# Cluster-masked attention and a maxout FFN: pairs of heads on two halves of the partitions, FFN blocks of 256 tokens

## The chip, the core and the metric

The kernel runs on one core of one Trainium2 chip. The core has five engines that run side by side, each through its own list of instructions in order: TensorE (PE) multiplies matrices, VectorE (DVE), ScalarE (ACT) and GpSimd (POOL) work element by element, and SyncE (SP) issues transfers to 16 DMA engines. PE writes to PSUM, in banks of 512 float32 columns; DVE and ACT read it. The metric is the time of one execution on the device in microseconds, lower is better.

## The reference, cut to what matters

```
B, H, S, D = 4, 8, 768, 64;  16 clusters;  FFN 512 -> 768 -> 512, three-way maxout
q_assign = argmax(q_n . c_n);  k_assign = argmax(k_n . c_n)        # per row and head
scores   = q k^T / sqrt(D), and -1e9 where q_assign != k_assign
attn     = exp(scores - max);  attn = attn / (sum + 1e-9)
x        = attn v, heads side by side                              # 3072 x 512
out      = max(x w1, x w2, x w3) w_out                             # weights are float64
```

## The kernel before, in words

Float32 products are split into parts so that PE's faster formats give nearly the whole precision: q and k into two float32r parts (`hi` and `lo`), probabilities, values, x and the hidden values into two float16 parts.

A pair of heads is prepared by `qk_prep`: both heads' q over k are loaded (q on the lower 64 partitions, k on the upper), ACT makes `hi` (L362), POOL or DVE makes `lo` (L365), and `qk_moves` shifts k's parts to the lower and q's to the upper half by DMA within SBUF (L370 to L372), so that one matmul over 128 partitions adds two products of parts. `cluster_scores` and `cluster_rows` find the cluster of each row and put one-hot rows below `q hi` and `k hi`, by DMA (L448).

The step of the attention is `scores`: one head, one tile of 128 queries. Two matmuls of 512 and 256 columns (L475), two more (L477), then a chain over engines: the row maximum on DVE (L480, written back scaled), the exponential with its row sum on ACT (L483), the factor 1/sum on DVE (L484, L485), the high part on ACT (L493) and the low part on DVE (L494). For some heads POOL splits instead (L489 to L491, chosen by `by_pool`). A DMA transpose turns both parts into `pt` (L495). There are 192 steps. `av` multiplies three tiles of `pt` with v (L505, L508), `x_split` makes two parts of x on POOL.

The FFN goes by blocks of 384 tokens (`ffn_units`): 18 groups of 12 matmuls (L546), whose results ACT and DVE fold into a maximum (L556, L558), POOL splits it (L564, L565), and three output tiles of 18 matmuls each (L580, L589, L591).

`spread` and `at_prio` give each piece a priority by the step it belongs to; a list scheduler puts the instructions of each engine into a fixed order by these. The first batch goes through its heads twice, half of the queries at a time, so that the FFN starts early; the FFN of a batch runs beside the attention of the next, the last one alone. The weights are converted from float64 on the chip (`convert`) during the first quarter of the program. PSUM holds three `big` tiles of two banks for scores and two `one` tiles of one bank for all else.

Of the kernel before, what the change touches and what calls it, by code (L numbers as in the profile page):

```python
# [8 lines left out]
F32 = mybir.dt.float32  # L9
# [7 lines left out]
AX = mybir.AxisListType  # L17
PSUM = bass.MemoryType.PSUM
# [5 lines left out]
def kernel(  # L24
# [23 lines left out]
    nc = tc.nc  # L48
    B, H, D, S = qk.shape
    D = D // 2  # L50
    C = cent.shape[0] // H
    P = 128
    QT = S // P
    NPAIR = H // 2
# [4 lines left out]
    G = 3  # L59
    AGAIN = {(0, 0), (1, 0)}  # L60
    NB = G * P
    NG = QT // G

# [4 lines left out]

    dpool = ctx.enter_context(tc.tile_pool(name="dr", bufs=2, space=bass.MemoryType.DRAM))
# [7 lines left out]
    def stage():  # L77
        return sb.tile([P, S], F32, tag="stage", name="stage", bufs=3)

# [1 line left out]
    fp = [ctx.enter_context(tc.tile_pool(name="ffn", bufs=2))]  # L81
    tctx = ExitStack()
    tp = tctx.enter_context(tc.tile_pool(name="first", bufs=1))
    ident = tp.tile([P, P], F32, name="ident")
# [6 lines left out]
    onehot = cpool.tile([P, S // 32, 32], F32, name="onehot")  # L91
    nc.gpsimd.memset(onehot, 0.0)
    cw = cpool.tile([P, H, P], F32R, name="cw")
    nc.gpsimd.memset(cw.bitcast(F32), 0.0)

    def pow2_scale(cols, name):
        """p: the power of two at or below the largest magnitude; s = 2^14 / p; on all partitions."""
# [13 lines left out]
    # A load that would run too far ahead is held back to the last step of the attention that  # L111
    # has been issued: one element of its tile is first written from the sums of that step.
    pace = []

    def hold(x):
        if pace:
            nc.gpsimd.tensor_copy(x, pace[-1])

    last = {}

    def behind(what, f, *args):
        with tc.issue_after(last[what].ins):
            f(*args)

# [6 lines left out]
    def centroids(c_sb):  # L131
# [3 lines left out]
        sq = tp.tile([P, D], F32, name="sq")  # L135
# [13 lines left out]
        c2 = tp.tile([P, 2, D], F32, name="c2")  # L149
# [4 lines left out]
        tv = t[:, 0:P].rearrange("p (h c) -> p h c", c=C)  # L154
        cv = cw.rearrange("p (r i) x -> p r i x", i=2)
        tv = tv.rearrange("p (r i) c -> p r i c", i=2)
        parts = []
        for a in range(2):
            rows = slice(D * a, D * a + D)
            for i in range(2):  # L160
                at = D * a + 32 * i
                parts.append((tv[rows, :, i, :], cv[rows, :, i, at : at + C], cv[rows, :, i, at + C : at + 2 * C]))
        for x, hi, lo in parts:
            last["cw_hi"] = nc.scalar.copy(hi, x)
        for x, hi, lo in parts:
            last["cw_lo"] = nc.vector.tensor_tensor(lo, x, hi.bitcast(F32), op=ALU.subtract)

# [8 lines left out]
    JA = 4  # L176
    w16 = [cpool.tile([P, JA, 2, 3, CT, P], F16, name="w16a")]
    wo16 = []
# [4 lines left out]
    top = [cpool.tile([P, DM], I32, name="top")]  # L183
    nc.gpsimd.memset(top[0], 0)

    def convert(wp, src, a, d):
        """src: int16 quarters of float64 in DRAM [P, a, 4m]; d: float32 [P, a * m] on chip."""
        n = d.shape[-1]
        x = wp.tile([P, n + 1, 4], I16, tag="wd", name="wd", bufs=2)
        hold(x[0:1, 0, 0:2].bitcast(F32))  # L190
        xf = x.rearrange("p n w -> p (n w)")
        nc.sync.dma_start(out=xf[:, 1 : 1 + 4 * n].rearrange("p (a m) -> p a m", a=a), in_=src)
        up = top[0]
        nc.scalar.copy(up.bitcast(F16).rearrange("p (n w) -> p n w", w=2)[:, 0:n, 1], x[:, 1:, 0].bitcast(BF16))
        low = x[:, 0:n, 2:4].bitcast(I32).rearrange("p n w -> p (n w)")
        nc.vector.scalar_tensor_tensor(
            d.bitcast(I32), low, 13, up[:, 0:n], op0=ALU.logical_shift_right, op1=ALU.bitwise_or
        )
# [10 lines left out]
    def w_units(wp, jt):  # L209
# [4 lines left out]
        def load(i):  # L214
            def f():
                if not i:
                    got["x"] = wp.tile([P, 3 * n], F32, tag="wf", name="wf", bufs=2)
                w = (w1, w2, w3)[i].bitcast(I16).rearrange("(c p) n -> p c n", p=P)
                src = w[:, :, 4 * jt * P : 4 * (jt + 1) * P]
                convert(wp, src, CT, got["x"][:, i * n : (i + 1) * n])  # L220
# [9 lines left out]
        def split(i):  # L230
            def f():
# [3 lines left out]
                    w16[jt // JA][:, jt % JA, 0, i].rearrange("p c n -> p (c n)"),  # L235
                    w16[jt // JA][:, jt % JA, 1, i].rearrange("p c n -> p (c n)"),
# [7 lines left out]
    def wo_units(fp):  # L244
        got = []

        def part(jt):
            def f():
                wp = fp[0]
                w = w_out.bitcast(I16)[jt * P : (jt + 1) * P, :]  # L250
                if jt % 3 == 0:
                    got[:] = [wp.tile([P, 3 * DM], F32, tag="wf", name="wf", bufs=2)]
                x = got[0][:, jt % 3 * DM : (jt % 3 + 1) * DM]
                convert(wp, w.rearrange("p (a n) -> p a n", a=1), 1, x)
# [8 lines left out]
                split16(x, s, wo16[0][:, jt, 0], wo16[0][:, jt, 1], WO_SPLIT[jt])  # L263
# [3 lines left out]
        def common():  # L267
# [9 lines left out]
            for jt in range(JT):  # L277
                t = wo16[0][:, jt].rearrange("p a n -> p (a n)")
# [6 lines left out]
    vmax = cpool.tile([P, B, NPAIR], F32, name="vmax")  # L285
    vsc = {}

    def v_max_units(b):
        def one_pair(pr):
            def f():  # L290
                x = stage()
                nc.sync.dma_start(out=x, in_=vv[b, :, 2 * pr : 2 * pr + 2].rearrange("p h t d -> p (h t d)"))
# [13 lines left out]
    def v_max_first():  # L306
        def part(i):
            def f():
                x = v_first[i] = fp[0].tile([P, 2 * S], F32, tag="vf", name="vf", bufs=2)
                h = H // 2  # L310
                nc.sync.dma_start(out=x, in_=vv[0, :, i * h : (i + 1) * h].rearrange("p h t d -> p (h t d)"))
# [13 lines left out]
    def v_prep(b, pr, loaded=False):  # L325
        if loaded:
            x = v_first[pr // 2][:, (pr & 1) * S : (pr & 1) * S + S]
        else:
            x = stage()
            nc.sync.dma_start(out=x, in_=vv[b, :, 2 * pr : 2 * pr + 2].rearrange("p h t d -> p (h t d)"))  # L330
        if loaded and V_SCALE[pr]:
            nc.scalar.activation(x, x, AF.Copy, scale=vsc[b][1])
        else:
            nc.gpsimd.tensor_scalar(x, x, vsc[b][1], 1.0, op0=ALU.mult, op1=ALU.mult)
        v = sb.tile([P, 2, QT, 2, D], F16, tag="v16", name="v16", bufs=4)
        xv = x.rearrange("p (h t d) -> p h t d", h=2, d=D)
        for h in range(2):
            nc.scalar.copy(v[:, h, :, h, :], xv[:, h])
            nc.gpsimd.tensor_tensor(v[:, h, :, 1 - h, :], xv[:, h], v[:, h, :, h, :], op=ALU.subtract)
        v16[b, pr] = v  # L340

# [1 line left out]
    # Rows of the input: q of a head over k of it. Per pair of heads:  # L343
    # [q lo; q hi], [q hi; onehot], [k hi; (onehot - 1) 2^100], [k hi; k lo].
    AQ, BQ, BK, AK = range(4)
    HALF = ((0, 512), (512, S))
    qkt = {}
    masks = {}

    def load(b, h):  # L350
        x = stage()
        nc.sync.dma_start(out=x, in_=qk[b, h])
        return x

    xin = {}

    def qk_prep(b, pr, i, pool, again=False):
        x = load(b, 2 * pr + i)
        if i == 0:
            qkt[b, pr] = pool.tile([P, 4, 2, S], F32R, tag="qk", name="qk", bufs=2 if pool is sb else 1)  # L360
        t = qkt[b, pr]
        last["hi"] = nc.scalar.copy(t[:, BQ, i], x)  # L362
        xin[i] = x
        eng = nc.vector if (b, pr) < (1, 1) and QK_LO[b * NPAIR + pr + (b == 0 and again) * (NPAIR + 1)] else nc.gpsimd
        last["lo"] = eng.tensor_tensor(t[:, AQ, i], x, t[:, BQ, i].bitcast(F32), op=ALU.subtract)  # L365

    def qk_moves(b, pr):
# [395 lines left out]
```

## Time and profile before

| | |
|---|---|
| time, median of 3 runs | 868.31 us (868.27 to 873.07) |
| span of the profiled execution, first to last instruction | 866.7 us (its own time is not given apart from that) |
| busy PE, DVE, ACT, POOL | 719.4, 611.4, 518.0, 494.4 us |
| mean granted TensorE clock | 0.915 of full speed |
| DMA moved | 149.86 MB, mean 173 GB/s |

A row of a group of instructions reads: line, engine, operation, what it writes and reads with sizes, count, then busy time and the mean duration in ns of one, then how long the engine sat idle just before them and which instruction ended most of that. PE's matmuls overlap each other, so that the distance of their starts, not their duration, is what one costs. A timeline row has start and length in us.

### The profile page before, as it was taken

Reading aid. Unit: us, or ns where it says so; the run is one execution under the profiler, and the core shown is the slowest. Engines: PE = TensorE matmul, PEld = TensorE weight load, DVE = VectorE, ACT = ScalarE, POOL = GpSimd, SP = SyncE. Lnnn points to the kernel's source line nnn. Section 1 sums busy time; section 2 is a strip of 40 time slices with the busy share of each in tenths; the row PEclk is TensorE's granted clock in tenths of the full one; section 3 lists DMA queues with packets and bytes.
Section 4 is the critical chain, followed back from the end, with each engine's and each line's share of the span. In section 5 each row is a group of like instructions: output and inputs, shape, how many; then the busy total and the mean of one; then the engine's idle time right before and its main releaser. Section 6 shows DMA issues by size and latency. Waiting matters only on the chain.

```text
span 866.7 us, 12102 instructions
## 1 busy us (share of the span) xinstructions
PE 719.4 (83%) x3836; PEld 422.7 (49%) x3836; DVE 611.4 (71%) x1327; ACT 518.0 (60%) x907; POOL 494.4 (57%) x486
## 2 busy tenths in 40 slices
PE   3445576767688998989898989989898999999997
PEld 2322343344354565545565545545555565556463
DVE  6777988798989898977798766876587667411020
ACT  6555668754867587868585756765767577510101
POOL 5687783583957374765786555785575446412111
PEclk9656576887889999999999999999999999999999
DMA  8999878999999999999999999897898676810100
GB/s 263 244 200 207 190 156 166 219 227 185 242 184 217 231 196 204 215 176 221 227 198 202 223 211 170 168 228 164 171 175 156 148 148 110 158 43 1 37 1 36
DMA packets 331263, 149.86 MB, mean 173 GB/s; under 512 B 304704, under 2 KB 313920, under 8 KB 331200
## 3 DMA queue, kind: packets, MB, share of 16 engines
q1 hardware_dynamic: 331200, 149.10, 83.2%
q8 instruction: 30, 0.49, 0.2%
q14 instruction: 33, 0.27, 0.1%
HBM read 38.57 MB, written 7.08 MB: 53 GB/s over the span
## 4 chain that ended last, share of the span: by engine, by line
PE 27%; DMA 19%; DVE 14%; ACT 9%; issue 7%; POOL 5%; SPq 2%; ACTq 0%; POOLq 0%; DVEq 0%
DMA pt<-hl 17%; PE one L546 13%; PE one L580 7%; DVE hl L494 5%; DVE big L480 4%; ACT e L483 3%; ACT hl L493 3%; PE one L505 2%; DMA stage<-in_v_dram 2%; POOL hl L491 2%; PE one L508 1%; PE big L475 1%; DVE onehot L434 1%; PE big L477 1%; SPq L495 1%
## 5 line engine op out<-in xcount | busy, mean ns | idle before, releaser
L494 DVE SCALAR_TENSOR_TENSOR hl<-e,r,hl 128x768 f16<-128x768 f32 x147 | 194.3, 1326 | 48.0 <-ACT hl L493 45.2
L546 PE MATMUL one<-x,w16a 128*128 128x384 f16 x1152 | 205.9, 332 | 18.2 <-DVE vf_h L558 9.8
L483 ACT ACTIVATE e<-big,nm 128x768 f32<-128x768 f32 x192 | 172.1, 897 | 77.4 <-DVE big L480 31.4
L480 DVE TENSOR_SCALAR_CACHE_REDUCE big<-big 128x768 f32<-128x768 f32 x192 | 181.8, 959 | 12.7 <-PE big L477 12.2
L493 ACT ACTIVATE hl<-e,r 128x768 f16<-128x768 f32 x147 | 135.9, 931 | 72.7 <-DMA pt<-hl 62.4
L475 PE MATMUL big<-qk 128*128 128x512 f32 (+1 forms) x384 | 128.0, 417 | 61.4 <-ACT e L483 59.6
L546 PEld LDWEIGHTS <-w16a 128*128 128x128 f16 x1152 | 110.2, 99 | 100.8 <-issue 36.1
L477 PE MATMUL big<-qk 80*128 80x512 f32 (+1 forms) x384 | 111.6, 374 | 15.5 <-DMA qk<-cl_t 12.7
L475 PEld LDWEIGHTS big<-qk 128*128 128x128 f32 x384 | 68.2, 209 | 96.0 <-ACT e L483 77.1
L546 PE MATMUL one<-x,w16b 128*128 128x384 f16 x576 | 101.8, 331 | 6.1 <-ACT xt L514 2.6
L505 PE MATMUL one<-pt,v 128*128 128x384 f16 x384 | 84.6, 358 | 17.3 <-DMA pt<-hl 9.1
L491 POOL TENSOR_TENSOR hl<-e,hl 128x768 f16<-128x768 f32 x45 | 77.6, 1730 | 27.6 <-ACT hl L490 27.1
L477 PEld LDWEIGHTS big<-qk 80*128 80x128 f32 x384 | 67.2, 212 | 28.2 <-issue 11.2
L546 PEld LDWEIGHTS <-w16b 128*128 128x128 f16 x576 | 55.1, 99 | 46.7 <-issue 13.7
L365 POOL TENSOR_TENSOR qk<-stage,qk 128x768 fp32r<-128x768 f32 x32 | 64.2, 2021 | 17.9 <-ACT qk L362 17.8
L518 POOL TENSOR_TENSOR xs<-xs,xt 128x384 f32<-128x384 f32 x32 | 34.7, 1084 | 61.9 <-ACT xt L514 61.9
L558 DVE SCALAR_TENSOR_TENSOR vf_h<-one,vf_h 128x384 f32<-128x384 f32 x48 | 26.4, 550 | 51.5 <-PE one L546 51.5
L505 PEld LDWEIGHTS <-v 128*128 128x128 f16 x384 | 37.1, 106 | 50.9 <-issue 24.9
L564 POOL TENSOR_SCALAR wf_h<-wf_h 128x384 f16<-128x384 f32 x24 | 15.5, 647 | 77.0 <-DVE wf_h L558 73.1
L489 POOL TENSOR_SCALAR e<-e,r 128x768 f32<-128x768 f32 x45 | 46.5, 1035 | 21.1 <-DVE r L485 9.6
L558 DVE SCALAR_TENSOR_TENSOR wf_h<-one,wf_h 128x384 f32<-128x384 f32 x48 | 26.5, 551 | 45.4 <-PE one L546 45.2
L490 ACT CAST hl<-e 128x768 f16<-128x768 f32 x45 | 37.2, 830 | 33.6 <-DMA pt<-hl 20.0
(130 smaller groups left out, 1042.8 us busy)
## 6 DMA issues: line engine op xcount, KB each, us to landing
stage<-in_qk_dram SPq DMA_DIRECT2D x36, 384.0 KB, 4.6
qk<-qk SPq DMA_DIRECT2D x16, 768.0 KB, 7.0
qk<-qk SPq DMA_DIRECT2D x32, 384.0 KB, 5.0
stage<-in_v_dram SPq DMA_DIRECT2D x25, 384.0 KB, 4.8
wd<-in_moe_w_dram SPq DMA_DIRECT2D x18, 512.0 KB, 4.6
out_dram<-o SPq DMA_DIRECT2D x24, 256.0 KB, 2.4
pt<-hl SPq DMA_TRANSPOSE x192, 4.3
wd<-in_moe_w_out_dram SPq DMA_DIRECT2D x6, 512.0 KB, 5.9
```

The costliest lines, as they stand in the source:

```text
L365: last["lo"] = eng.tensor_tensor(t[:, AQ, i], x, t[:, BQ, i].bitcast(F32), op=ALU.subtract)
L475: nc.tensor.matmul(t[:, lo:hi], aq[:, qs], ak[:, lo:hi], start=True, stop=False)
L477: last["pe"] = nc.tensor.matmul(t[:, lo:hi], bq[0:K2, qs], bk[0:K2, lo:hi], start=False, stop=True)
L480: last["nm"] = nc.vector.tensor_scalar(e, e, -SCALE, 3.0e38, op0=ALU.mult, op1=ALU.min, accum_out=nm)
L483: nc.scalar.activation(x, e, AF.Exp, bias=nm, scale=-1.0, accum_out=r)
L491: nc.gpsimd.tensor_tensor(hl[:, 1, :], x, hl[:, 0, :], op=ALU.subtract)
L493: nc.scalar.activation(hl[:, 0, :], x, AF.Copy, scale=r)
L494: nc.vector.scalar_tensor_tensor(hl[:, 1, :], x, r, hl[:, 0, :], op0=ALU.mult, op1=ALU.subtract)
L505: nc.tensor.matmul(t[:, 0:NB], vt, pt[:, :, kt, :], start=(kt == 0), stop=False)
L546: nc.tensor.matmul(t[:, 0:NB], w16[jt // JA][:, jt % JA, wa, i, ct], x16[b, gi, ct][:, xa, :], start=(n == 0), stop=(n == 3 * CT - 1),)
L558: nc.vector.scalar_tensor_tensor(m, t[:, 0:NB], 2.0**-24, ms[jt], op0=ALU.mult, op1=ALU.max)
L580: nc.tensor.matmul(t[:, 0:DM], h16[jt][:, ha, tt * P : (tt + 1) * P], wo16[0][:, jt, wa, :], start=(n == 0), stop=(n == 3 * JT - 1),)
```

## The change

The kernel is rewritten around pairs of heads.

- The input holds the pair's two heads on the lower and upper 64 partitions, for q and for k. `qk_prep` loads a pair in one piece and splits it with one ACT and one POOL (or DVE) operation of 1536 columns. There are no moves between partitions and no rows inside q and k.
- `attend` handles both heads of a pair at one query tile: 96 steps. Each head's products use 64 rows of PE's array: hi hi, lo hi, hi lo, and as a fourth one the one-hot rows against the mask, in bfloat16. The heads alternate matmul by matmul. The maximum is a plain reduction that leaves PSUM as it is, with a small scaling behind it. ACT makes all high parts and DVE all low parts; POOL has none. One transpose serves both heads.
- `cluster_rows` treats two pairs at once and leaves the one-hot rows in tiles of their own.
- `av` writes head 0 to the lower and head 1 to the upper 64 partitions of one PSUM tile (column tiles); ACT and DVE make the two parts of x directly from it.
- FFN blocks have 256 tokens: 12 blocks. All weights have places of their own from the start; they are converted in steps 0 to 18 of 96. Buffers: two for e (three before), two for hl of twice the size, one for loaded q and k, three `wide` ones that v, weights and hidden values share.
- The tables that chose between engines, and the paced loads, are gone.

```
+    def attend(b, pr, qt, pt, g):
+        ts = [big() for h in range(2)]
+        with together():
+            for k in range(4):
+                for lo, hi in HALF:
+                    for h in (1, 0):
+                        rows = slice(D * h, D * h + D)
+                        if k == 3:
+                            w, m = oh[rows, 0, qs], km[rows, pr & 1, lo:hi]
+                        else:
+                            w, m = x[rows, int(k == 1), 0, qs], x[rows, int(k == 2), 1, lo:hi]
+                        nc.tensor.matmul(ts[h][:, lo:hi], w, m, start=(k == 0), stop=(k == 3))
+                        now()
+        for h in range(2):
+            nc.vector.tensor_reduce(nm, t, axis=AX.X, op=ALU.max, negate=True)
+            nc.vector.tensor_scalar_mul(nm, nm, SCALE)
+            e = sb.tile([P, S], F32, tag="e", name="e", bufs=EBUFS)
+            nc.scalar.activation(e, t, AF.Exp, bias=nm, scale=SCALE, accum_out=r[:, h : h + 1])
+        nc.vector.tensor_scalar(r, r, 1.0e-9, 2.0**-14, op0=ALU.add, op1=ALU.mult)
+        nc.vector.reciprocal(r, r)
+        hl = sb.tile([P, 2, 2, S], F16, tag="hl", name="hl", bufs=2)
+        for h in range(2):
+            nc.scalar.activation(hl[:, h, 0], es[h], AF.Copy, scale=r[:, h : h + 1])
+            nc.vector.scalar_tensor_tensor(hl[:, h, 1], es[h], r[:, h : h + 1], hl[:, h, 0], ...)
+        nc.sync.dma_start_transpose(out=pt[:, g], in_=hl.rearrange("p h a s -> p (h a s)"))
...
+    def av(b, pr, gi, pt):
+        todo = [(kt, va, pa) for kt in range(QT) for va, pa in HLS]
+        with together():
+            for n, (kt, va, pa) in enumerate(todo):
+                for h in range(2):
+                    nc.tensor.matmul(t[D * h : D * h + D, 0:NB], v[:, va, h * QT + kt, :],
+                        pt[:, :, (2 * h + pa) * QT + kt, :], ...)
+                    now()
+        nc.scalar.activation(x[:, 0, :], t[:, 0:NB], AF.Copy, scale=2.0**-14)
+        nc.vector.scalar_tensor_tensor(x[:, 1, :], t[:, 0:NB], 2.0**-14, x[:, 0, :], ...)
...
-    G = 3
+    G = 2
-    def qk_moves(b, pr):
-        nc.sync.dma_start(out=t[up, BK : AK + 1], in_=t[dn, BQ : BQ + 1].broadcast_to([D, 2, 2, S]))
-    W_A, W_B, W_O = (4, 33), (30, 43), (38, 52)
+    W_A, W_O = (0, 14), (10, 18)
+    EBUFS = 2
```

`together` has the scheduler keep PE's instructions of a group in the order written, `now` sets the priority of what is left of a group to the highest.

**DVE in the later batches, before.** `big` is a head's scores, `r` its factor, `hl` its parts; the numbers tell the heads apart.

```order
L480 TENSOR_SCALAR big_5032,nm_5037<-big_5032 128x768
L480 TENSOR_SCALAR big_5070,nm_5075<-big_5070 128x768
L484 TENSOR_SCALAR r_5039<-r_5039 128x1
L485 RECIPROCAL r_5039<-r_5039 128x1
L480 TENSOR_SCALAR big_5108,nm_5113<-big_5108 128x768
L558 SCALAR_TENSOR_TENSOR wf_h_4792<-one_4813,wf_h_4792 128x384
L480 TENSOR_SCALAR big_5139,nm_5144<-big_5139 128x768
L484 TENSOR_SCALAR r_5077<-r_5077 128x1
L485 RECIPROCAL r_5077<-r_5077 128x1
L494 SCALAR_TENSOR_TENSOR hl_5044<-e_5040,r_5039,hl_5044 128x768
```

The maxima of three later heads (5070, 5108, 5139) stand between the first head's maximum and its low part. **DVE in the later batches, now:** the end of one step, the whole next one and the start of a third; here `nm` is a head's maximum.

```order
L435 SCALAR_TENSOR_TENSOR hl_7495<-e_7491,r_7482,hl_7495 128x768
L425 TENSOR_REDUCE nm_7614<-big_7592 128x1
L425 TENSOR_REDUCE nm_7619<-big_7593 128x1
L426 TENSOR_SCALAR nm_7614<-nm_7614 128x1
L426 TENSOR_SCALAR nm_7619<-nm_7619 128x1
L430 TENSOR_SCALAR r_7613<-r_7613 128x2
L431 RECIPROCAL r_7613<-r_7613 128x2
L489 SCALAR_TENSOR_TENSOR m_7529<-one_7516,m_7514 128x256
L435 SCALAR_TENSOR_TENSOR hl_7626<-e_7617,r_7613,hl_7626 128x768
L435 SCALAR_TENSOR_TENSOR hl_7626<-e_7622,r_7613,hl_7626 128x768
L425 TENSOR_REDUCE nm_7685<-big_7663 128x1
```

The maxima of a step stand behind the low parts of the step before. **ACT at the same place, now:**

```order
L434 ACTIVATE hl_7495<-e_7491,r_7482 128x768
L521 ACTIVATE o_7435<-one_7416,so_1_2_4719 128x512
L521 ACTIVATE o_7457<-one_7438,so_1_2_4719 128x512
L428 ACTIVATE e_7617,r_7613<-big_7592,nm_7614 128x768
L428 ACTIVATE e_7622,r_7613<-big_7593,nm_7619 128x768
L487 ACTIVATE m_7514<-one_7501 128x256
L434 ACTIVATE hl_7626<-e_7617,r_7613 128x768
L434 ACTIVATE hl_7626<-e_7622,r_7613 128x768
```

Both exponentials of a step stand behind both high parts of the step before. **DVE ahead of the first row maximum, before:** the last rows of the first pair's clusters, then the first head.

```order
L434 TENSOR_TENSOR onehot<-rank,cl_m_172 128x24x16
L435 TENSOR_SCALAR onehot<-onehot 64x24x16
L438 STREAM_TRANSPOSE cl_t<-onehot 128x768
L446 CAST qk<-cl_t 16x768 x2
L480 TENSOR_SCALAR big,nm<-big 128x768
```

The first head's maximum follows the clusters directly. **The same place now;** `wd` are loaded weights, `wf` converted ones, `wmx` their maxima.

```order
L379 TENSOR_TENSOR onehot_93<-rank_74,cl_m2_171 128x48x16
L103 TENSOR_SCALAR sc_m_512<-sc_m_512 128x1
L185 SCALAR_TENSOR_TENSOR wf_578<-wd_666,top_105 128x512
L381 STREAM_TRANSPOSE oh_178<-onehot_93 128x1536
L104 TENSOR_SCALAR sc_m_512<-sc_m_512 128x1
L185 SCALAR_TENSOR_TENSOR wf_578<-wd_670,top_105 128x512
L384 TENSOR_SCALAR km_180<-oh_178,selbig_95 128x768 x2
L211 TENSOR_REDUCE wmx_2_202<-wf_578 128x1
L185 SCALAR_TENSOR_TENSOR wf_824<-wd_825,top_105 128x512
L425 TENSOR_REDUCE nm_229<-big_207 128x1
```

Ten conversions of weights (L185) now stand ahead of the first maximum; none did before.

More of the change, by code (lines that the diff above doesn't have):

```diff
@@ L328, in v_prep @@
         else:
[L329 to L339, printed above, removed]
+            x = sb.tile([P, S], F32, tag="vs", name="vs", bufs=2)
@@ new lines, in qk_prep @@
+    def qk_prep(b, pr):
+        x = sb.tile([P, 2, S], F32, tag="stage", name="stage", bufs=1)
+        nc.sync.dma_start(out=x, in_=qk[b, pr])
+        t = qkt[b, pr] = sb.tile([P, 2, 2, S], F32R, tag="qk", name="qk", bufs=3)
+        hi, lo = (t[:, a].rearrange("p a s -> p (a s)") for a in range(2))
+        xf = x.rearrange("p a s -> p (a s)")
+        nc.scalar.copy(hi, xf)
+        eng = nc.vector if (b, pr) in LO_VECTOR else nc.gpsimd
+        eng.tensor_tensor(lo, xf, hi.bitcast(F32), op=ALU.subtract)
@@ new lines, in cluster_rows, with together @@
+        nc.vector.transpose(out=oh.rearrange("p a s -> p (a s)"), in_=onehot.rearrange("p n c -> p (n c)"))
+        km = sb.tile([P, 2, S], BF16, tag="km", name="km", bufs=2)
+        for j in range(2):
+            nc.vector.tensor_scalar(
+                km[:, j], oh[:, 1], 1.0, selbig[:, j : j + 1], op0=ALU.subtract, op1=ALU.mult
+            )
+        masks[b, d] = oh, km
+    @contextmanager
+    def together():
+        p = tc.cur_priority
+        with tc.manual_schedule(engines={PE}):
+            yield
+        tc.cur_priority = p + 100
```

473 lines of the change are left out of this document (167 added, 306 removed).

## The prediction

> **What bounds the kernel now.** I read the page's busy line first, then the busy time by stage, then the chain that ended last.
>
> ```profile
> PE 719.4 (83%) x3836; PEld 422.7 (49%) x3836; DVE 611.4 (71%) x1327; ACT 518.0 (60%) x907; POOL 494.4 (57%) x486
> 0.00:240.00 240.00, 145.04 (x563) 84.97 (x565) 198.04 (x412) 151.66 (x262) 159.96 (x174) 0.73 0.94 209
> 240.00:414.00 174.00, 156.40 (x869) 92.77 (x864) 151.67 (x342) 126.29 (x223) 104.75 (x94) 0.97 1.03 205
> 414.00:588.00 174.00, 154.89 (x895) 93.59 (x894) 133.03 (x298) 118.37 (x210) 118.18 (x106) 0.99 1.00 204
> 588.00:760.00 172.00, 161.98 (x936) 95.51 (x935) 115.32 (x256) 108.53 (x191) 91.94 (x86) 0.99 0.81 153
> 760.00:866.00 106.00, 101.09 (x582) 55.91 (x580) 13.38 (x24) 13.12 (x24) 19.52 (x27) 1.00 0.06 21
> PE 27%; DMA 19%; DVE 14%; ACT 9%; issue 7%; POOL 5%; SPq 2%; ACTq 0%; POOLq 0%; DVEq 0%
> L480 DVE TENSOR_SCALAR_CACHE_REDUCE big<-big x192: 928/955/1006, 21.6 to 737.9; 128x768 f32<-128x768 f32 x192
> ```
>
> The stage rows give length, then busy time of PE, weight loads, DVE, ACT and POOL, granted clock, DMA share and GB/s. The first batch (to 240 us) is full on no engine: weights are converted there, and PE's clock stands at 0.73. The three later batches take some 173 us each with PE busy 155 to 162 and DVE 115 to 152. Then comes a tail of 106 us, PE alone. No engine owns the chain: PE has 27% of it, DMA 19, DVE 14. So the kernel lives on overlap, above all of one head's row maxima with another head's splits. The row of L480, the first DVE operation of each head, says how well: from 21.6 to 737.9 us for 192 heads, 716.3/191 = 3.75 us a head or **7.5 us a pair**. Whatever the change does to busy times, its pace per pair is to be set against that.
>
> **The path of a step after the change.** A step is now two heads at one query tile, 96 steps. DVE, as the order in the section on the change shows, has for each step: two maxima (L425), two small scalings (L426), then r (L430, L431), then the two low parts (L435), and only then the next step's maxima. ACT's rows stand equally strictly: two exponentials, two high parts. In the order before, the maxima of two later heads stand between a head's maximum and its split. So the handoffs DVE-ACT-DVE-ACT-DVE, hidden now, lie on the path. The prices:
>
> ```profile
> L494 DVE SCALAR_TENSOR_TENSOR hl<-e,r,hl 128x768 f16<-128x768 f32 x147 | 194.3, 1326 | 48.0 <-ACT hl L493 45.2 <-DMA pt<-hl 1.4 <-issue 0.7
> L494 DVE SCALAR_TENSOR_TENSOR hl<-e,r,hl x147: 976/1020/5728, 30.7 to 750.1; 128x768 f16<-128x768 f32 x147
> L485 DVE RECIPROCAL r<-r 128x1 f32<-128x1 f32 x192 | 29.2, 157 | 2.9
> L484 DVE TENSOR_SCALAR r<-r 128x1 f32<-128x1 f32 x192 | 27.4, 145 | 35.2 <-ACT e L483 34.7
> L293 DVE TENSOR_REDUCE vmax<-stage 128x1 f32<-128x768 f32 x12 | 11.3, 947 | 7.4 <-DMA stage<-in_v_dram 7.4
> L483 ACT ACTIVATE e<-big,nm 128x768 f32<-128x768 f32 x192 | 172.1, 897 | 77.4 <-DVE big L480 31.4 <-DVE hl L494 22.5 <-DVE r L484 8.5
> L493 ACT ACTIVATE hl<-e,r 128x768 f16<-128x768 f32 x147 | 135.9, 931 | 72.7 <-DMA pt<-hl 62.4 <-issue 4.2 <-DVE hl L494 2.1
> 507.07 0.13 DVE L480 DVE_READ_ACCUMULATOR big<-big 128x1 f32 x1
> 507.30 0.90 ACT L483 ACTIVATE e<-big,nm 128x768 f32<-128x768 f32 x1 [2.79 <-DVE big L480]
> 508.10 0.19 ACT L483 ACTIVATION_READ_ACCUMULATOR e<-big,nm 128x1 f32 x1
> 508.33 0.15 DVE L484 TENSOR_SCALAR r<-r 128x1 f32<-128x1 f32 x1 [1.12 <-ACT e L483]
> 508.51 0.16 DVE L485 RECIPROCAL r<-r 128x1 f32<-128x1 f32 x1
> ```
>
> The maximum over 768 columns of PSUM has no row; the nearest are L293, the same reduction from SBUF, 0.947, and L480 itself, 0.955. Two are 1.90, and the first scaling 0.15 (as L484). The timeline shows an exponential with its sum from 507.30 to 508.29, 1.0; two are 2.0. r with both operations is 0.31. The first high part is 0.93. The two low parts at their median are 2.04; the second high part runs beside the first of them. Handoffs: 507.20 to 507.30 from DVE to ACT, 508.29 to 508.33 back; four of them, 0.3. Sum: 1.90 + 0.15 + 2.0 + 0.31 + 0.93 + 2.04 + 0.3 = **7.6 us a step**, 730 us for 96. Before anything else is added the bare chain already fills the 7.5 us that a pair takes now.
>
> **What DVE does besides.**
>
> ```profile
> L558 DVE SCALAR_TENSOR_TENSOR vf_h<-one,vf_h 128x384 f32<-128x384 f32 x48 | 26.4, 550 | 51.5 <-PE one L546 51.5
> L480 DVE TENSOR_SCALAR_CACHE_REDUCE big<-big 128x768 f32<-128x768 f32 x192 | 181.8, 959 | 12.7 <-PE big L477 12.2
> L196 DVE SCALAR_TENSOR_TENSOR wf<-wd,top 128x512 int32<-128x512 int32 x24 | 22.7, 944 | 10.2 <-ACT top L194 10.0
> L434 DVE TENSOR_TENSOR onehot<-rank,cl_m 128x384 f32<-128x384 f32 x16 | 17.6, 1100 | 0.1
> 0.00:866.00 866.00, 67.24 (x84) 33.01 (x32) 0.92 0.84 173
> L312 DVE TENSOR_REDUCE vmax<-vf 128x1 f32<-128x1536 f32 x2 | 3.5, 1752 | 1.4 <-DMA vf<-in_v_dram 1.3
> L365 DVE TENSOR_TENSOR qk<-stage,qk x2: 958/958/958, 5.4 to 7.0; 128x768 fp32r<-128x768 f32 x2
> ```
>
> By L558 (384 columns, 0.550) and L480 (768, 0.959) a column costs 1.07 ns, so the maxout over 256 columns costs 0.41. In the loop there are some 112 of these (48 of the 144 fall into the tail), 46 us, and 48 new low parts of x16, 20 us, which POOL did. The cluster rows: the windows row is what touches cl_t, DVE 67.24, with L434 and its neighbour about 94 for 16 pairs; the new ones take two pairs at once, the same elements, so 82 for the seven pairs of pairs behind the first. The 14 conversions, maxima and splits of weights that come after the first step cost about 28, maxima of v and scales 18. Together 194 us. The holes of the chain, while ACT does the exponentials and the first high part, are 2.9 us a step. Counting in the order which rows stand in a hole and which between the low parts and the next scaling, about half lie outside: **100 us** on the path. The bounds are 60 (those outside meet a wait anyway) and 194.
>
> **Stretching: 45 us.** The low part has a median of 1.020 and a mean of 1.326. POOL gives up its 45 of 192 heads and its part in x16, so I take half of that excess, 0.13 x 192 = 25; then 20 us for ACT's other rows in the chain and for PE bursts. Bounds 0 and 59 + 40.
>
> **The start.** Before the first maximum DVE's order now has ten weight conversions (9.4 us), six maxima over v (two by L312, four by L293, 7.3), two low parts of 1536 columns (by L365, 3.8), three maxima over weights (as L312, 5.3), the first cluster rows for two pairs (14) and some 35 small operations (5): 45 us from 5.4 us on, with waits for 10 MB of loads **53 us** instead of 21.6. Bounds 45 and 75.
>
> **PE and the moves.** The moves between partitions go: 48 transfers. Their DMA time was hidden in part; the transposes carry the same bytes in half as many pieces, and hl's two buffers leave a piece two steps, 18 us, to land. I price both at nothing; if the larger pieces don't land in that time, each is worth at most the excess over 18 us.
>
> ```profile
> 503.01 1.14 PE L505 MATMUL one<-pt,v 128*128 128x384 f16 x6
> 504.07 0.68 PE L508 MATMUL one<-pt,v 128*64 128x384 f16 x6
> 504.68 0.62 PE L475 MATMUL big<-qk 128*128 128x512 f32 x2
> 506.20 2.13 PE L546 MATMUL one<-x,w16a 128*128 128x384 f16 x12
> 752.05 10.32 PE L580 MATMUL one<-wo,wf_h 128*128 128x512 f16 x47
> 839.70 10.40 PE L546 MATMUL one<-x,w16b 128*128 128x384 f16 x63
> DMA to landing us min/median/max: 3.6/4.3/10.5
> ```
>
> Long runs: 10.40/63 = 0.165 us for 384 columns, 10.32/47 = 0.220 for 512, so 0.110 for 256: FFN blocks of 256 cost 216 x 0.110 + 36 x 0.220 = 31.7 us, 12 of them as much as 8 of 384. The six matmuls of L508 write alternate column halves and take 0.61 us, not 0.99: column tiles run two at a time, and about 0.11 of that is the change of shape. Scores of two heads took 506.20 - 504.68 = 1.52. With the row halves two at a time the streamed columns are the same; each half loads its own weights, so I take 1.9, between 1.5 (nothing lost) and 3.2 (one after the other, and two changes). A step of PE in the later batches is then 1.9, half of an av of 18 x 0.11 + 0.2, 1.1, an eighth of a block, 4.0, and 0.3 for changes: 7.3 of the 9.1 us that DVE's chain takes ((730 + 100 + 45)/96). The next scores can begin when the first exponential has freed its bank, 4.5 us before the next maximum; PE stays covered.
>
> That change of shape is also a rule of the Trainium skill, TensorEngine Tiling (Array Packing), section Tiling Modes: switching the mode drains the array. The 0.11 us agrees with it. The new order has 510 such switches among its 6370 matmuls, before 150 among 3832; by the rule laid open it would add 40 us, an estimate, and the sum would be 1050. The same section says that tiles of one mode run in parallel; no run here shows that for rows, and by it the scores stay near 1.5.
>
> **The tail.** After the last low part: the transpose lands (4.3 for 1536 columns; 7 for 3072), av 2.2, x16 0.8 and then, by the order, 108 output and 432 hidden matmuls: 108 x 0.220 + 432 x 0.110 = 71 us, less what runs while the transpose lands is nothing here, plus 2.4 for the last store: 83. It was 866.7 - 751.1 = 116, since more FFN was left over.
>
> **Sum:** 53 + 730 + 100 + 45 + 83 = **1011 us** against the profile's span of 866.7. The median of the runs, 868.31, is 1.6 above that span, so 1012.
>
> **Rivals.**
> - *The row halves don't run together* (the change doesn't do what it says). Then PE needs 1.3 us more a step, 8.6 of 9.1, its cover is gone and every burst of FFN delays a maximum; I reckon 10.1 us a step, 1011 + 96 = about 1105. For it: no row tile is in the trace, and each matmul here loads its own weights. Against: the column halves of L508.
> - *The chain is looser than I think*: the start takes 45, the other DVE work hides to 60, nothing stretches: 45 + 730 + 60 + 0 + 80 = 915.
> - *Faster*: the steps overlap after all. If DVE worked without holes, a step would be the larger of DVE's own (1.9 + 0.3 + 0.31 + 2.04 + 194/96 = 6.6) and PE's 7.3: 96 x 7.3 + 53 + 83 = 837. It decides below (868 - 136)/96 = 7.6 us a step with all extras in. For it speak POOL's relief and the moves that go; against it DVE's own order, which can't be overtaken.
>
> **How the numbers follow.** The serial chain (960 to 1060): 0.62. Row halves one after the other (1060 to 1150): 0.22. Looser (890 to 960): 0.11. Faster: 0.03, and 0.01 within 1% (about what a measurement of this kernel can tell from no change). The range leaves out the faster case and the outer parts of its neighbours: 930 to 1110.
>
> **What would show it.** In the new profile: from first to last L425 some 875 us at 9.1 a step, the first at 53; DVE idle before L430 for ACT e and before L435 for ACT hl in nearly every step, which together are over 150 us; L425 waiting little for PE; low parts near 1.1; PE busy under 80% until the tail of 80 us. If L425 waits for PE in most steps, the row halves are serial. I would be wrong if DVE's idle time before L430 and L435 were small.

## The result, and the profile after

The changed kernel takes **1039.7 us** (median of 4 runs, 1038.6 to 1041.0) against 869.9 us before on the same chips (868.3 to 873.1): ratio **1.195**, 95% interval 1.192 to 1.199. The forecast was 1012 in a range of 930 to 1110. The profiled span is 1037.9 us.

First the page's busy line:

```profile
PE 822.8 (79%) x6428; PEld 577.5 (56%) x6428; DVE 636.3 (61%) x1247; ACT 472.4 (46%) x810; POOL 252.9 (24%) x277
```

Then the busy time by stage (length, PE, weight loads, DVE, ACT, POOL, granted clock, DMA share, GB/s):

```profile
50.00:300.00 250.00, 159.75 (x1010) 103.74 (x1012) 168.33 (x354) 116.44 (x196) 70.42 (x62) 0.72 0.55 122
300.00:500.00 200.00, 164.38 (x1309) 114.53 (x1307) 124.19 (x246) 98.32 (x168) 44.09 (x40) 0.86 0.60 125
500.00:700.00 200.00, 168.76 (x1378) 118.29 (x1374) 132.49 (x256) 104.85 (x180) 47.15 (x40) 0.91 0.59 122
```

And the row maxima (times of one in ns, first and last start):

```profile
L425 DVE TENSOR_REDUCE nm<-big x192: 920/948/959, 50.4 to 914.7; 128x1 f32<-128x768 f32 x192
```

DVE is busier by 25 us, ACT and POOL are relieved, DMA moves less, and yet none of DVE, ACT and POOL is full in any of these stages. The row of L425 says where the 171 us between the spans are: the first maximum comes at 50.4 instead of 21.6 us (29 more), the 192 maxima take 864.3 instead of 716.3 us (148 more), and behind the last one there are 123.2 instead of 128.8 (6 fewer). From the first maximum of one step to that of the next it is 863.5/95, so a pair of heads now takes **9.1 us instead of 7.5**.

A clean step, from the timeline (start and length in us):

```profile
354.31 1.81 DVE L425 TENSOR_REDUCE nm<-big 128x1 f32<-128x768 f32 x2
...
356.04 0.14 DVE L426 TENSOR_SCALAR nm<-nm 128x1 f32<-128x1 f32 x1
...
356.29 0.90 ACT L428 ACTIVATE e<-big,nm 128x768 f32<-128x768 f32 x1 [2.79 <-DVE nm L426]
...
357.19 0.89 ACT L428 ACTIVATE e<-big,nm 128x768 f32<-128x768 f32 x1
...
358.20 0.17 DVE L430 TENSOR_SCALAR r<-r 128x2 f32<-128x2 f32 x1 [1.12 <-ACT e L428]
358.40 0.17 DVE L431 RECIPROCAL r<-r 128x2 f32<-128x2 f32 x1
358.65 1.76 ACT L434 ACTIVATE hl<-e,r 128x768 f16<-128x768 f32 x2 [0.48 <-ACT e L428]
359.62 1.95 DVE L435 SCALAR_TENSOR_TENSOR hl<-e,r,hl 128x768 f16<-128x768 f32 x2 [1.05 <-ACT hl L434]
```

Nearly every row starts within 0.1 us or so of the end of the one before; only the first low part (359.62) starts when the first high part is done, beside the second. From the maxima at 354.31 to the end of the low parts at 361.57 are 7.26 us. The waits of DVE show the same over the whole run (total, times, longest):

```profile
DVE r L430 <- ACT e L428: 123.7, 81, 2.7
DVE m L489 <- PE one L477: 94.9, 53, 10.0
DVE hl L435 <- ACT hl L434: 71.8, 79, 1.8
DVE nm L425 <- PE big L418: 50.2, 12, 13.0
```

Of the wait for the FFN (L489), 83 of the 95 us lie in the tail; inside the loop it is 12.

But the steps are not all like that. The distances of the 96 first maxima have a median of 7.9 us (7.5 in the three later batches), and 17 of the 95 are over 10, up to 21.4. One of the longest, the step whose maximum comes at 111.76:

```profile
96.08 2.34 PE L449 MATMUL one<-pt,v 128*64 128x256 f16 x20 [8.96 <-DMA pt<-hl]
...
98.36 0.79 PE L418 MATMUL big<-qk 64*128 64x512 f32 x1
...
99.08 0.42 PE L449 MATMUL one<-pt,v 128*64 128x256 f16 x1
99.43 0.58 PE L418 MATMUL big<-qk 64*128 64x256 f32 x1
...
99.94 0.42 PE L449 MATMUL one<-pt,v 128*64 128x256 f16 x1
...
100.29 0.58 PE L418 MATMUL big<-qk 64*128 64x256 f32 x1
...
111.76 0.96 DVE L425 TENSOR_REDUCE nm<-big 128x1 f32<-128x768 f32 x1 [9.84 <-PE big L418]
```

PE first stands 8.96 us for a transpose, then issues av's matmuls and those of the next scores one by one in turn, 0.67 to 1.08 us a pair, for 13 us, while DVE waits 9.84. `together` keeps the order within a group, but not two groups apart when both have the highest priority. Seven of the 96 score groups have 22 or more such alternations; from first to last matmul they take 133.6 us, the waits inside them included.

The price of a pair goes with PE's clock, as the stage rows of such stretches show:

```profile
98.30:111.70 13.40, 13.40 (x33) 5.36 (x31) 2.91 (x3) 1.53 (x2) 0.00 (x0) 0.50 0.48 119
618.00:623.00 5.00, 5.00 (x27) 2.49 (x21) 2.89 (x4) 1.76 (x2) 1.82 (x3) 1.00 0.71 202
623.00:628.00 5.00, 5.00 (x13) 1.89 (x12) 0.00 (x0) 0.00 (x0) 0.00 (x0) 0.52 1.14 165
```

The first is the stretch above, all of it at a granted clock of 0.50. The other two are one stretch of alternation, from 618.5 us on: for its first 4.7 us the clock is 1.00 and a pair takes 0.53 to 0.66 us, then the clock falls to 0.50 and a pair takes 0.67 to 0.95. In the whole run 32 such pairs ran at clock 1.00 (median 0.58) and 74 at 0.50 (median 0.86).

### The profile page after: what moved, and what is told of

The parts are those of the page before. It is cut to its first block, busy times and chain, and to the rows that moved or that the text cites. A ratio compares the mean times of both kernels' runs of the same rounds, so it can differ in the third digit from the quotient of the medians.

```text
span 1037.9 us, 16289 instructions
## 1 busy us (share of the span) xinstructions
PE 822.8 (79%) x6428; PEld 577.5 (56%) x6428; DVE 636.3 (61%) x1247; ACT 472.4 (46%) x810; POOL 252.9 (24%) x277
## 5 line engine op out<-in xcount | busy, mean ns | idle before, releaser
L477 PE MATMUL one<-x,w 128*128 128x256 f16 x2592 | 312.2, 277 | 32.8 <-DVE nm L426 15.4
L477 PEld LDWEIGHTS <-w 128*128 128x128 f16 x2592 | 250.6, 99 | 93.8 <-issue 58.5
L418 PE MATMUL big<-qk 64*128 64x512 f32 (+1 forms) x1152 | 229.3, 411 | 79.3 <-ACT e L428 75.3
L435 DVE SCALAR_TENSOR_TENSOR hl<-e,r,hl 128x768 f16<-128x768 f32 x192 | 205.5, 1101 | 72.1 <-ACT hl L434 71.8
L418 PEld LDWEIGHTS big<-qk 64*128 64x128 f32 x1152 | 139.8, 211 | 138.0 <-ACT e L428 89.7
L425 DVE TENSOR_REDUCE nm<-big 128x1 f32<-128x768 f32 x192 | 174.5, 948 | 50.2 <-PE big L418 50.2
L449 PE MATMUL one<-pt,v 128*64 128x256 f16 x1728 | 151.0, 300 | 46.0 <-DMA pt<-hl 39.2
L449 PEld LDWEIGHTS <-v 128*64 128x64 f16 x1728 | 106.7, 119 | 93.1 <-issue 62.6
L489 DVE SCALAR_TENSOR_TENSOR m<-one,m 128x256 f32<-128x256 f32 x144 | 60.5, 420 | 97.0 <-PE one L477 94.9
L512 PE MATMUL one<-wo,h 128*128 128x512 f16 x432 | 98.9, 384 | 4.7 <-DVE nm L426 3.5
L430 DVE TENSOR_SCALAR r<-r 128x2 f32<-128x2 f32 x96 | 23.5, 244 | 123.8 <-ACT e L428 123.7
L418 PE MATMUL big<-km,oh 64*128 64x512 bf16 (+1 forms) x384 | 82.3, 375 | 11.8 <-DVE km L384 11.8
```

The costliest lines, as they stand in the source:

```text
L418: nc.tensor.matmul(ts[h][:, lo:hi], w, m, start=(k == 0), stop=(k == 3))
L425: nc.vector.tensor_reduce(nm, t, axis=AX.X, op=ALU.max, negate=True)
L435: nc.vector.scalar_tensor_tensor(hl[:, h, 1], es[h], r[:, h : h + 1], hl[:, h, 0], op0=ALU.mult, op1=ALU.subtract)
L449: nc.tensor.matmul(t[D * h : D * h + D, 0:NB], v[:, va, h * QT + kt, :], pt[:, :, (2 * h + pa) * QT + kt, :], start=(n == 0), stop=(n == l ...
L477: nc.tensor.matmul(t[:, 0:NB], w16[:, jt, wa, i, ct], x16[b, gi, ct][:, xa, :], start=(n == 0), stop=(n == 3 * CT - 1),)
L489: nc.vector.scalar_tensor_tensor(m, t[:, 0:NB], 2.0**-24, box["m"], op0=ALU.mult, op1=ALU.max)
```

## The experiments

Theory: the softmax chain, serial in the order of the instructions, sets the step. Rivals: PE's time, the moves (transposes), the order of PE's groups. Times are medians, of two runs in the first four experiments and in the loop without FFN, of four or five in the others; in brackets stand the ratio to the kernel before and its interval. The kernel before, run beside them, took 869.7 to 871.1.

**A shorter chain.** Maximum and scaling in one instruction, as before the change.

```
-            nc.vector.tensor_reduce(nm, t, axis=AX.X, op=ALU.max, negate=True)
-            nc.vector.tensor_scalar_mul(nm, nm, SCALE)
+            nc.vector.tensor_scalar(t, t, -SCALE, 3.0e38, op0=ALU.mult, op1=ALU.min, accum_out=nm)
```

> The row maximum and its scaling are again one DVE operation (min of -t/8 with an accumulated result, the scaled scores written back), so that the first exponential need not wait for the second maximum and two scalings. Nothing else changes; DVE's busy time stays within 10 us. If the DVE-ACT chain of a step is the pace (theory), about 1.05 us leaves each of 96 steps: the time between first and last maximum falls from 864 to about 765, the total to 930 to 960. If PE is the pace (rival), it stays between 1020 and 1045.

Measured 1029.8 (ratio 1.183, 1.172 to 1.194). That is outside the theory's 930 to 960 and inside the rival's 1020 to 1045. The least distance of two steps fell from 6.4 us (7.2 in an undisturbed step) to 3.9 and the median of the later batches from 7.5 to 6.9, so the chain was what held the short steps. The total hardly moved: 29 steps are now over 10 us, 17 before. The waits name a new one, which is not among those of the changed kernel:

```profile
ACT e L427 <- DVE big L425: 120.2, 64, 6.0
...
ACT hl L433 <- DMA pt<-hl: 71.9, 20, 5.7
```

ACT waits for a buffer of `hl` that a transpose still reads. So the chain holds the undisturbed steps, but it is refuted as the whole explanation: of the some 100 us that it was to give back, 10 came.

**Less work for PE.** Hidden groups of the first three batches with 4 matmuls instead of 12.

```
+                if b < B - 1:
+                    todo = todo[::3]
```

> Leaves work out: in the FFN of the first three batches each hidden group has 4 matmuls in place of 12, with the same evacuations; PE has about 2 us less to do in each step of the last three batches. Theory (serial chain): PE was covered, first to last maximum falls by the 50 us at most that maxima wait for PE, total 985 to 1035. Rival (PE is the pace): 72 steps lose about 2 us each, total below 910.

Measured 1056.8 (1.214, 1.205 to 1.222): PE's busy time fell from 823 to 759 us and the kernel got slower. Neither expectation came, but the rival is out: the amount of PE's work isn't the bound. The 1296 matmuls left out would be 143 us at 0.110 each (an estimate by the price at full clock); the busy time fell by 64 only, since the granted clock fell from 0.87 to 0.78 and 0.80 in the two runs and the matmuls that were left took longer.

**Row halves in turn.** Head 0's eight matmuls, then head 1's.

```
-            for k in range(4):
-                for lo, hi in HALF:
-                    for h in (1, 0):
+            for h in (0, 1):
+                for k in range(4):
+                    for lo, hi in HALF:
```

> All eight matmuls of head 0, then all eight of head 1, so that two row halves never run at the same time and a step's scores cost PE about 2.7 us in place of 1.4. But head 0 is ready earlier, and in the order of DVE the next step's first maximum now stands ahead of the low parts in many steps. If PE is the pace, about 1.3 us more in each step, total 1120 to 1170. If the handoffs are the pace, the staggering shortens the chain by up to one maximum and one low part a step: total 930 to 1020.

Measured 1045.3 (1.201, 1.181 to 1.220; the two runs are 1038.3 and 1052.4), no change that can be told, and neither expectation.

**Head 1 split by POOL.**

```
+            if h:
+                nc.gpsimd.tensor_scalar(es[h], es[h], r[:, h : h + 1], 1.0, op0=ALU.mult, op1=ALU.mult)
+                nc.scalar.copy(hl[:, h, 0], es[h])
+                nc.gpsimd.tensor_tensor(hl[:, h, 1], es[h], hl[:, h, 0], op=ALU.subtract)
+                continue
```

> Head 1's probabilities are scaled and split by POOL with ACT (as L489 to L491 did), head 0's as now: one low part of 1.0 us leaves DVE in each step, POOL gets 2.8. Theory (serial chain): the next maxima stand one low part earlier, 0.9 us a step less, total 940 to 990, unless ACT's copy for head 1, which waits for POOL, delays the next exponentials and eats it. Rival (PE): 1025 to 1045.

Measured 1056.1 (1.213, 1.206 to 1.220). Neither expectation came. DVE lost 67 us of busy time and the time grew: neither is DVE's amount of work the bound. But head 1's parts now pass through POOL (0.91 and 1.64 us) and ACT in turn, so this run doesn't test a shorter chain.

**Whole groups.** av's matmuls less urgent than those of the scores.

```
         # in av
-                    now()
+                    tc.cur_priority = 50
```

> The changed kernel with one edit: the matmuls of an av group take a lower urgency than those of a score group, so that the two are no longer issued one by one in turn; each score group's 16 matmuls stand together in PE's order. Everything is computed. In the changed kernel seven groups of scores alternate with av's matmuls 22 times or more and take 25.0, 25.1, 19.7, 17.5, 20.2, 12.1 and 14.0 us, 133.6 us in all. Theory 'alternation' (each pair of one av and one score matmul takes 0.9 to 1.1 us where the same matmuls in whole groups take 0.2): these steps fall to some 7.5 us each, 52.5 in all, and the time to about 960 us (940 to 985). Rival 'late transposes' (PE waits in those steps for the transposed probabilities, in whatever order its matmuls stand): within 15 us of 1040. Rival 'chain' (the softmax chain sets the loop, the rest lies in its holes): within 20 us of 1040, and the least distance of two steps stays 7.2 us.

Measured **985.2** (1.133, 1.129 to 1.136), 54.5 us less, at the edge of the 940 to 985 expected from alternation: alternation is real, two thirds of its estimate. DVE's wait for the scores, the price of alternation, has all but gone from the row of L425:

```profile
L425 DVE TENSOR_REDUCE nm<-big 128x1 f32<-128x768 f32 x192 | 174.4, 948 | 5.7 <-PE big L418 5.7
```

That it was the alternation, and not scores held up behind a late transpose, shows in the step from above, where all is alike up to the end of PE's wait:

```profile
95.98 2.34 PE L449 MATMUL one<-pt,v 128*64 128x256 f16 x19 [8.95 <-DMA pt<-hl]
98.25 2.06 PE L418 MATMUL big<-qk 64*128 64x512 f32 x10
...
100.26 0.50 PE L418 MATMUL big<-km,oh 64*128 64x256 bf16 x3
100.69 1.17 PE L449 MATMUL one<-pt,v 128*64 128x256 f16 x17
...
101.79 1.81 DVE L425 TENSOR_REDUCE nm<-big 128x1 f32<-128x768 f32 x2
```

PE waits for the transpose as long as before (8.95 us), and the scores still stand behind the first of av's matmuls; but what took 13.3 us in turn takes 3.6 in groups, and the maximum comes at 101.79 instead of 111.76. Over the whole run PE's waits for transposes fall by 8 us only (matmuls of av, 39.2 to 30.9).

In time order PE changes between score, av and full-array matmuls 510 times in the changed kernel and 338 times here, 0.32 us for each change saved. An estimate from the pairs comes out alike: the 109 alternating pairs took 89.8 us, at the price of whole groups at the same clock they would take some 24, so 66 us less. The median step stays at 7.7 (7.5 in the later batches), as the chain wants.

**Whole groups and the short chain.**

> The edit before (av and score groups whole) together with the short chain (maximum and scaling in one instruction). Everything is computed. Alone, the short chain brought 10 us, while its least distance of two steps fell from 7.2 to 3.9 us; its mixed groups took 193 us in all. If alternation ate that gain: 15 mixed groups at some 5 us instead of 13, another 110 us less than 1030, so 900 to 940. If late transposes or the coupling through the evacuations of PE's accumulators ate it: 1000 to 1030, with steps of over 10 us as before.

Measured 973.8 (1.118, 1.115 to 1.122): again only 11 us for the shorter chain, and ACT's wait for `hl` is there again, 75.7 us. Neither the 900 to 940 expected from alternation came nor the 1000 to 1030 of its rival.

**The same with the heads in turn.**

> The two edits before, and each step's first head computed whole before the second (8 matmuls, then 8), so that the row halves of TensorE no longer run side by side but the first head can use the one free accumulator early. Everything is computed. If the wait of the scores for a free accumulator (the exponential of the step before) is what is left: 20 to 50 us less than the run with the two edits. If TensorE's time is what is left: 96 steps by some 1.2 us more, 60 to 115 us more than that run.

Measured 990.7 (1.139, 1.134 to 1.145): 17 us slower. That is neither expectation; side by side the row halves are worth something, but less than the PE time they save.

**The loop without FFN** (on whole groups).

```
+                if b == B - 1:
                     spread(ffn_units(b, gi), a, z, F_LATE)
```

> The kernel with whole groups, without the FFN of the first three batches (their output is not written; only the last batch's three blocks are computed, in the tail). If the softmax chain sets the loop: the 72 steps of the later batches stand at 7.2 to 7.6 us but for the cluster rows, so about 600 us instead of the 700 between 283 and 862 less... in numbers: distance of first maxima of steps 24 and 95, 579 us in the kernel with whole groups, becomes 540 to 570, and DVE's wait for L430 and L435 behind ACT stays over 170 us. If the FFN's use of PE and its evacuations lengthen the steps beyond that: under 520. If the transposes set it: unchanged within 10.

Measured 1010.2 (1.161, 1.153 to 1.168), slower than with the FFN; steps 24 to 95 took 613 us. None of the three expected distances came; only DVE's wait behind ACT stayed, as the chain wants (235 us). Most steps are at 7.2 and 7.5, and about every fourth at 10 to 12:

```profile
714.38 1.76 ACT L434 ACTIVATE hl<-e,r 128x768 f16<-128x768 f32 x2 [0.48 <-ACT e L428]
715.35 1.95 DVE L435 SCALAR_TENSOR_TENSOR hl<-e,r,hl 128x768 f16<-128x768 f32 x2 [1.05 <-ACT hl L434]
716.05 3.59 PE L449 MATMUL one<-pt,v 128*64 128x256 f16 x31 [8.84 <-DMA pt<-hl]
719.58 1.61 PE L418 MATMUL big<-qk 64*128 64x512 f32 x10
...
721.68 1.82 DVE L425 TENSOR_REDUCE nm<-big 128x1 f32<-128x768 f32 x2 [4.39 <-PE big L418]
```

PE stands at av for a transpose, the next scores stand behind av, and DVE waits for those. The granted clock was 0.69 and 0.73 in the stages from 300 and 500 us, with PE 53 and 52% busy; the kernel with whole groups has 0.89 and 0.97 there, with PE 78 and 87% busy. The Trainium skill, TensorE: Matmul & The Clock Gate, Part 1, says that PE's activity releases its throttle; this run agrees (PE 53% busy from 300 us on), so the late scores are slower too. How much of the 25 us over the kernel with whole groups is the clock, and how much av's place in PE's order, isn't separated.

**Plain copies instead of transposes** (on whole groups and short chain).

```
-        nc.sync.dma_start_transpose(out=pt[:, g], in_=hl.rearrange("p h a s -> p (h a s)"))
+        nc.sync.dma_start(out=pt[:, g], in_=hl.rearrange("p h a (t n) -> p (h a t) n", n=P))
```

> The kernel with whole groups and the short chain, its 96 transposes replaced by plain copies of the same bytes from the same queue (so av multiplies untransposed probabilities). There ACT waits 75.7 us for buffers that a transpose still reads, and steps alternate between 4 and 10 to 19 us. If the transposes (3.6 us to issue, 5.5 to land, two buffers) ate the gain of the short chain: those waits go and the time falls from 974 to 900 to 935. If TensorE, 87 to 92% busy in the later batches, is the bound by now: within 12 us of 974.

Measured **925.0** (1.063, 1.058 to 1.068), 49 us less than 973.8 and within the expectation of the transposes. ACT's wait for `hl` halves:

```profile
ACT hl L433 <- DMA pt<-hl: 37.2, 17, 5.1
```

So once the chain is short, the transposes are one of the limits, worth 49 us. What they cost shows in the queue's own rows; the kernel before the change:

```profile
L495 SPq DMA_TRANSPOSE pt<-hl x192: 1277/1814/7436, 33.5 to 755.5; - x192
```

and the changed kernel:

```profile
L438 SPq DMA_TRANSPOSE pt<-hl x96: 3520/3621/5802, 60.0 to 921.5; - x96
```

A transpose of twice the bytes holds SP's queue 3.62 us instead of 1.81, and lands after 5.5 (median) instead of 4.3; two steps share one `pt`, so av can't begin before both have landed. A plain copy holds the queue 0.47 us and lands after 3.6. Whether it is the queue, the landing or the buffers held until then, this run doesn't tell.

**Each head's chain by itself** (on the kernel with heads in turn, whole groups and short chain): scores, maximum, exponential, factor, high and low part of one head, then the other's.

> The kernel with whole groups, the short chain and the heads in turn (990.7 us), and in it each head's chain written by itself: scores, maximum, exponential, factor, high and low part of one head, then of the other, so that in DVE's order maxima of a later head stand ahead of the low parts of an earlier one, as in the kernel before the change. Everything is computed. If it is the lockstep of the two heads that holds the loop: 900 to 950. If TensorE with the row halves in turn, or the transposes, hold it: within 12 us of 991.

Measured 989.9 (1.135, 1.128 to 1.142) against 990.7: no change, although maxima of later heads now stand ahead of earlier low parts. So undoing the lockstep alone gives nothing, once the heads are in turn. ACT waits 83.5 us for `hl` here and 93.3 us in the kernel it is compared with, which fits the transposes as the limit; PE with the row halves in turn isn't excluded.

**av a step later**, with the long and with the short chain.

```
-    AV_LAG, AV_LATE = 1, 1
+    AV_LAG, AV_LATE = 2, 2
```

> The kernel with whole groups (985.2 us), with av placed one step later in PE's order (AV_LAG and AV_LATE 2 instead of 1), so that a transpose has a step more to land before PE reaches the matmuls that read it. Everything is computed. In the loop without FFN every fourth step took 11 to 12 us, because PE stood at an av up to 12.9 us for its transposes with the next scores behind it. If that wait is what is left above the chain's 7.2 to 7.5 us: more steps at 7.2 to 7.5 and a time of 945 to 970. If the two buffers of pt then hold the transposes back instead: within 10 us of 985, or slower.

> The same with the short chain too (973.8 us with av at its old place). Everything is computed. With plain copies in place of transposes that kernel took 925. If av's wait for a transpose is the larger part of what the transposes cost: 930 to 955. If it is the buffers hl and pt that they hold: within 12 us of 974.

Measured 985.5 (1.133, 1.128 to 1.138) and 999.3 (1.147, 1.140 to 1.154): no gain, as expected of the buffers, then a loss of 25 us, which neither expectation had. With the short chain ACT's wait for `hl` grows from 75.7 to 95.3 us, and SP's waits at the transposes that PE's hidden groups end from 113.8 to 152.6. That fits two buffers of `pt` that come free a step later, with transposes that wait for them.

No version came below the kernel before.

## Why the prediction was right, and where it was not

| part | predicted | measured |
|---|---|---|
| to the first maximum | 53 | 50.4 |
| 96 steps to the last low part | 875 | 871.0 |
| behind it | 83 | 116.5 |
| span | 1011 | 1037.9 |

- **The chain** was right as the pace of an undisturbed step: 7.6 us predicted, 7.2 to 7.5 measured, with DVE's waits before L430 and L435 at 195 us ("over 150"). The run with the short chain moved these steps. It isn't what one gains by shortening it: 10 us instead of some 100, since longer steps took their place. And 7.2 to 7.5 us is no more than the pair took before (7.5); what made the loop slower lies on top. (Between a head's maximum and its low part the order before has the maxima of three later heads, not two as the prediction says; its argument stays.)
- **What comes on top** (145 us) was near in its sum and wrong in its content. At 7.3 us a step the measured loop has 170 us on top; with whole groups 118. So some 52 us were alternation, which the sum priced at nothing. That the loop came within 4 us of its 875 is luck: the chain was taken 29 us too long and the rest 25 us too short. The sentence on the Trainium skill, TensorEngine Tiling (Array Packing), section Tiling Modes, priced its 510 switches at 40 us more. For this term that was the better estimate; the trace agrees that a change costs time. But the price was 0.32 us a change, three times the 0.11 of the trace of before, and was paid where matmuls alternate one by one, mostly at half the clock. The total of 1050 by that rule proves nothing: its loop would be 915, and 871 was measured.
- **The low part's stretching**: mean 1.101, median 1.014, so 17 us in 192; 25 were taken for it. (Half of the excess of 0.306 would have been 0.15 a head and 29 us, not 0.13 and 25.)
- **The moves** were priced at nothing with two steps, 18 us, to land. They do land in time for `hl`, but av needs two of them, and PE waited for that 39 and 26 us (matmuls, weight loads). In this kernel that is a part of the long steps (the two waits run beside each other); with a short chain, plain copies in their place give back 49 us.
- **The tail** is the term that was mis-sized: 83 against 116.5. The sum counted 108 output and 432 hidden matmuls; the timeline has 144 and 708:

```profile
922.83 6.72 PE L477 MATMUL one<-x,w 128*128 128x256 f16 x60
929.49 2.16 PE L449 MATMUL one<-pt,v 128*64 128x256 f16 x36
931.57 7.94 PE L512 MATMUL one<-wo,h 128*128 128x512 f16 x36
939.35 23.74 PE L477 MATMUL one<-x,w 128*128 128x256 f16 x216
962.93 7.93 PE L512 MATMUL one<-wo,h 128*128 128x512 f16 x36
```

The last two rows come three times. Their prices were right: 23.74/216 = 0.110 and 7.93/36 = 0.220. The first 60 hidden matmuls run while the last transpose lands: av starts 8.0 us after the last low part, where the sum had 7. Of the rest the sum left out one block, 216 hidden and 36 output matmuls, 31.7 us: the last batch has three blocks, and it counted two. The tail is as long as before the change (115.5 us there). The error of 33.5 us is more than the whole difference between 1011 and 1038.
- **The rival on row halves** was wrong: L425 waits for PE 12 times. At clock 1.00, 16 score matmuls that stand together take 1.4 us from first to last start (median of 15 groups, in which the two heads' matmuls mostly start 0.01 us or less apart; 1.9 assumed), and 2.2 with the heads in turn (median of 20). So the row halves do run side by side.
- **The DMA** gets no term in the prediction, though its own stage rows have the DMA share at 0.94 to 1.03 up to 588 us, more than any engine's. The changed kernel has 0.55 to 0.60 in the stages shown. What that relief was worth, no run shows.
- **The faster rival** needed steps without holes; the order didn't allow it, as argued. But the run with each head's chain by itself, on the heads in turn, shows that there the order alone doesn't bring it either.

What stays open is how the other 118 us on top of the chain divide among cluster rows, weight conversions (the first 24 steps take 232 us with whole groups, later ones 196 on average), and PE's waits for transposes: no run separates these. Nor does a run show what the first maximum, 29 us later than before, costs by itself. More buffers for `hl` or `pt` weren't tried.

## What to carry to other kernels

Two heads in lockstep turn a pipeline over three score tiles into a chain DVE-ACT-DVE-ACT-DVE; add up that chain first and compare it with the pace of the kernel before. Where it only equals that pace, everything that disturbs a step is loss, and shortening the chain brings little until the disturbances are gone. Then look in PE's order for groups of different tile shapes that are issued in turn, and give one of them the lower priority: here one line was worth 54 us. Count what stands behind the last dependent row matmul by matmul before pricing a tail.

## What was not expected of the hardware

- A matmul pair alternating between row tiles (64x128) and column tiles (128x64) costs 0.53 to 0.66 us at a granted clock of 1.00, where whole groups take 1.4/15 = 0.09 for a score matmul and 2.16/36 = 0.06 for one of av; at a clock of 0.50 it costs 0.67 to 1.08.
- In the alternation from 618.5 us on the clock fell from 1.00 to 0.50 after 4.7 us, in that from 885.5 us after 3.9, although the profile has PE busy without a gap. So the busy share alone doesn't tell the clock.
- Taking PE work away lowered its granted clock (0.69 and 0.73 in the loop without FFN, 0.89 and 0.97 with it), and the kernel was slower by 25 us.
- A transpose of 768 KB, twice the size, keeps its issuing queue busy twice as long (3.62 against 1.81 us), so that half as many transposes save that queue nothing: 96 x 3.62 = 348 us, 192 x 1.81 = 348.
